# Loads of the up weights: from ScalarE's DMA queue to SyncE's

## The chip, the cores and the metric

The kernel runs on one core of a Trainium2 chip. The metric is the device time in microseconds (us) of one execution. Engines are named as in the profile: PE is TensorE, DVE is VectorE, ACT is ScalarE, POOL is GpSimd, SP is SyncE. SP does no arithmetic here; it issues DMA transfers. ACT computes and can issue DMA transfers as well. "SPq" and "ACTq" mark what an engine's sequencer does, such as issuing a transfer.

## What is computed

The reference has two parts: a causal linear attention with decay, and a two-layer network on its output.

```
# q, k, v: (4, 8, 768, 64) float32; lam: (8,)
for b in range(seq // 64):                      # blocks of 64 tokens
    intra = einsum('bhic,bhjc->bhij', qb, kb) * Dmask        # Dmask = lam ** (i - j), causal
    intra = einsum('bhij,bhjd->bhid', intra, vb)
    inter = einsum('bhid,bhde->bhie', qb * lam_pow, kv_state)
    out[:, :, block] = intra + inter
    kv_state = lam_block * kv_state + einsum('bhsd,bhse->bhde', kb * rev_pow, vb)
x = out.transpose(0, 2, 1, 3).reshape(3072, 512)
h = x @ w_in                                    # w_in: (512, 2048)
return maximum(0.01 * h, h) @ w_out             # w_out: (2048, 512)
```

w_in and w_out come in as 64-bit floats, everything else as 32-bit floats. "Up" is the product with w_in, "down" the product with w_out.

## The kernel before

**Attention.** Tokens are handled in 24 rounds of 128 (two blocks of the reference). A round loads k, q and v (`load_kq` L330, `load_v` L374), transposes k and q on PE (L391), copies the transposes out of PSUM on ACT (L402 for k, L403 for q), multiplies q and k by powers of lam (L411, L407), forms scores and the state update on PE (psc, by the helper at L312), masks the scores on DVE (L440), adds the state (L445, L447) and forms the output (po, again L312). The output is then split into three numbers, `xh`, `xl` and `xm` (L495 to L498), because the later products are made of three fast passes. k, q and v have two buffers each, so a load of round c + 2 waits for the PE work of round c. In the early rounds PE also makes filler transposes (`busy`, L265), a fixed number that the planner inserts.

**Weights.** The columns of w_in are taken in eight panels of 256. Each panel comes in two halves of 512 KB, so there are 16 loads; they go in turn into three staging buffers `raw`. Panels are taken in the order 1, 0, 2, 3, 7, 6, 5, 4, so loads 1 and 2 are panel 1, 3 and 4 panel 0, 5 and 6 panel 2. `to_float32` (L544) converts a half from 64 to 32 bits: its `get` issues the load, three ACTIVATEs (L566, L568, L570) read the staging buffer, and two DVE operations (L572, L573) put the words together in `w32`. `parts` (L575) then splits the panel into `wh`, `wl` and `wm` (L579 or L581, L584, L590). A staging buffer is free again when its three ACTIVATEs are done. The same function loads w_out later, from SP's queue.

**Up and down.** `up` (L616) multiplies a group of 512 tokens by a panel in three passes (L628), corrects and applies the leaky ReLU on ACT (L646, L649), and stores the result in device memory (L652, `g<-gs`). When all is done, `down` reads it back and makes the second product (L688).

**Order of the work.** The order on each engine isn't written by hand. `Plan` (L37) holds every operation with an estimated duration and its dependences, simulates the engines together with one resource "DMA", and emits the operations in order of their planned start. A load is planned on "DMA" by `move` (L278); which engine's queue issues it is settled only in the function that is then called. An engine works through its instructions in the emitted order. Transfers that SP issues go into SP's queue, those that ACT issues into ACT's queue.

Transfers take eight completion counters in turn, over both queues. A transfer waits on its issuing engine until the former transfer on its counter has landed; it also waits for the last reader of what it overwrites.

Of the kernel before, what the change touches and what calls it, by code (L numbers as in the profile page):

```python
# [36 lines left out]
class Plan:  # L37
# [23 lines left out]
    def add(self, eng, us, fn, reads=(), writes=(), rank=0.0):  # L61

        n, deps = len(self.ops), set()
        for k in reads:
            w, r = self.last.setdefault(k, [None, []])
            if w is not None:
                deps.add(w)
            r.append(n)
        for k in writes:
            w, r = self.last.setdefault(k, [None, []])  # L70
            if w is not None:
                deps.add(w)
            deps.update(r)
            self.last[k] = [n, []]
        deps.discard(n)
        ways = {eng: us} if isinstance(eng, str) else dict(zip(eng, us))
        if self.slack:
            self.more[n] = self.slack
        if self.chain is not None:
            self.chains[self.chain].append(n)  # L80
        self.ops.append((ways, fn, deps, (self.rank + rank, n), set(writes)))
# [81 lines left out]
def kernel(  # L163
# [10 lines left out]
    nc = tc.nc  # L174
# [103 lines left out]
    def move(us, fn, reads, writes, issue=0.5, rank=0.0, slack=SLACK):  # L278

        plan.slack = slack if steady else EARLY_SLACK  # L280
        if steady and not rank:
            rank = FIRST
        add("DMA", length(us, issue), fn, reads, writes, rank=rank)
        plan.slack = 0.0
# [259 lines left out]
    def to_float32(kind, p, h, dst, key, after=()):  # L544

        nonlocal n_raw
        j, n_raw = n_raw % (1 if kind == "wo" else len(raw)), n_raw + 1
        r, low, kl = raw[j], lows[n_raw % 2], f"low{n_raw % 2}"
        d = dst.bitcast(I32)

        def get():
            r64 = r.bitcast(I64)
            if kind == "wi":
                nc.scalar.dma_start(out=r64.rearrange("p (k f) -> p k f", k=2),
                                  in_=w_in_r[:, 2 * h:2 * h + 2, p * 2 * P:(p + 1) * 2 * P])
            else:
                nc.sync.dma_start(out=r64, in_=moe_w_out[(2 * p + h) * P:(2 * p + h + 1) * P, :])

        def words(i, dt):
            return r.bitcast(dt).rearrange("p (n two) -> p n two", two=2)[:, :, i]  # L560

        def addend(dt, i):
            return low.bitcast(dt).rearrange("p (n two) -> p n two", two=2)[:, :, i]

        move(1.6, get, after, [f"raw{j}"])
        add("ACT", 0.67, lambda: nc.scalar.activation(out=dst, in_=words(1, F32), func=AF.Abs, scale=2.0 ** -110),  # L566
            [f"raw{j}"], [key])
        add("ACT", 0.78, lambda: nc.scalar.activation(out=addend(U16, 0), in_=words(0, U32), func=AF.Copy, bias=0.0, scale=2.0 ** -29),  # L568
            [f"raw{j}"], [kl])
        add("ACT", 0.77, lambda: nc.scalar.activation(out=addend(F16, 1), in_=words(1, F32), func=AF.Copy, bias=0.0, scale=2.0 ** -100),  # L570
            [f"raw{j}"], [kl])
        add("DVE", 0.42, lambda: nc.vector.tensor_scalar(d, d, 3, None, op0=ALU.logical_shift_left), [], [key])  # L572
        add("DVE", 1.0, lambda: nc.vector.tensor_tensor(d, d, low, op=ALU.add), [kl], [key])  # L573
# [230 lines left out]
```

## Time and profile before

| what | value |
|---|---|
| median of 3 runs | 612.86 us (612.70 to 613.33) |
| the profiled execution's own time | 614.14 us |
| its span, first to last instruction | 612.3 us |
| PE busy | 600.5 us, 98% of the span |
| DVE, ACT, POOL busy | 312.2, 270.9, 83.0 us |
| moved by DMA | 104.66 MB, 171 GB/s on average |
| the 16 loads of w_in | issued from 7.0 to 79.0 us, 374 ns median to issue, 4.0 to 6.4 us to land |

A row of the profile names a group of instructions: line, engine, operation, output <- input, sizes and count. In the order of time a row begins with its start and duration in us; in brackets at its end stands how long the engine had been idle before and what ended that. Matmuls are pipelined and their ends are modelled. "Landing" is the end of a transfer, counted from the start of its issue. The chain that ended last is followed back from the last instruction, at each step to what released it. The names of tiles leave buffer numbers out: `raw` is any of the three staging buffers, and `att` is one large tile that holds nearly all of the attention's buffers.

### The profile page before, as it was taken

How to read it: one execution, taken by the hardware profiler on the slowest of the kernel's cores; microseconds unless marked ns; L12 is line 12 of the kernel's file. 1: busy time of each engine (PE TensorE's matmuls, PEld its weight loads, DVE VectorE, ACT ScalarE, POOL GpSimd, SP SyncE). 2: the span in 40 equal slices, each digit the busy share in tenths (PEclk: the TensorE clock that was granted, in tenths of full speed). 3: DMA queues.
4: the chain of work that ended last, by engine and by line, in shares of the span. 5: the costliest groups of instructions: out<-in, count | busy, mean ns of one | idle time of the engine just before them, and what ended most of it. 6: DMA issues, size and time to landing. Idle time of an engine off the chain costs nothing.

```text
span 612.3 us, 12915 instructions
## 1 busy us (share of the span) xinstructions
PE 600.5 (98%) x5402; PEld 498.1 (81%) x5402; DVE 312.2 (51%) x412; ACT 270.9 (44%) x434; POOL 83.0 (14%) x90
## 2 busy tenths in 40 slices
PE   8899999999999999999999999999999999999997
PEld 6677888888888888888788888888888888888886
DVE  3899981064353344326356845535454554635531
ACT  2778884444465655556577522221222313214111
POOL 1563410053233013103000000000000000000000
PEclk9999999999999999999999999999999999999999
DMA  9999876544889969876776842523433343433201
GB/s 205 219 248 255 237 205 169 152 123 131 192 207 253 234 192 244 219 237 172 287 263 223 286 161 88 187 70 126 149 101 122 120 135 106 138 103 121 86 1 69
DMA packets 141162, 104.66 MB, mean 171 GB/s; under 512 B 117040, under 2 KB 117808, under 8 KB 141104
## 3 DMA queue, kind: packets, MB, share of 16 engines
q1 hardware_dynamic: 136608, 95.44, 53.7%
q10 hardware_dynamic: 4496, 8.39, 4.5%
q8 instruction: 42, 0.69, 0.5%
q14 instruction: 16, 0.13, 0.1%
HBM read 68.16 MB, written 35.65 MB: 170 GB/s over the span
## 4 chain that ended last, share of the span: by engine, by line
PE 93%; DVE 4%; DMA 1%; POOL 1%; issue 0%; SPq 0%; ACT 0%; DVEq 0%; ACTq 0%; POOLq 0%
PE b L628 41%; PE b L688 18%; PE po L688 11%; PE psc L688 11%; PE po L312 4%; PE pt L688 4%; PE psc L312 3%; DVE w L572 1%; DVE w L573 1%; DMA att<-in_v_dram 1%; PE pt L391 1%; DVE wm L590 0%; DVE att L447 0%; DVE wl L584 0%; DVE wh L581 0%
## 5 line engine op out<-in xcount | busy, mean ns | idle before, releaser
L670 ACT ACTIVATE xh<-att 128x1024 fp32r<-128x1024 f32 x48 | 50.9, 1061 | 147.1 <-PE b L688 145.4
L671 DVE SCALAR_TENSOR_TENSOR xl<-att,xh 128x1024 fp32r<-128x1024 f32 x48 | 58.7, 1223 | 99.0 <-ACT xh L670 99.0
L628 PE MATMUL b<-xl,wl 128*128 128x512 f32 (+1 forms) x392 | 102.9, 386 | 0.6 <-DVE wl L584 0.6
L628 PE MATMUL b<-xh,wh 128*128 128x512 f32 (+1 forms) x392 | 102.7, 386 | 0.8 <-ACT xh L495 0.8
L628 PE MATMUL b<-xm,wm 128*128 128x512 f32 (+1 forms) x392 | 103.2, 391 | 0.0
L628 PEld LDWEIGHTS b<-xh,wh 128*128 128x128 f32 x392 | 72.7, 188 | 16.1 <-ACT xh L495 0.9
L628 PEld LDWEIGHTS b<-xl,wl 128*128 128x128 f32 x392 | 72.5, 188 | 15.7 <-DVE wl L584 1.0
L628 PEld LDWEIGHTS b<-xm,wm 128*128 128x128 f32 x392 | 71.3, 188 | 14.6
L649 ACT ACTIVATE gs<-b 128x512 f32<-128x512 f32 x96 | 57.2, 597 | 47.9 <-PE b L628 44.1
L646 ACT ACTIVATE b<-b 128x512 f32<-128x512 f32 x96 | 56.0, 585 | 50.4 <-PE b L628 50.3
L688 PE MATMUL b<-wl,xl 128*128 128x512 f32 x192 | 74.7, 389 | 0.0
L688 PE MATMUL b<-wh,xh 128*128 128x512 f32 x192 | 74.7, 389 | 0.0
L673 DVE SCALAR_TENSOR_TENSOR xm<-xl,xh 128x1024 fp32r<-128x1024 f32 x48 | 58.8, 1226 | 5.1 <-DVE xl L671 0.5
L440 DVE TENSOR_TENSOR att<-psc,att 128x512 f32<-128x512 f32 x24 | 16.5, 689 | 64.6 <-PE psc L312 64.5
L688 PEld LDWEIGHTS b<-wl,xl 128*128 128x128 f32 x192 | 36.1, 188 | 7.5
L688 PEld LDWEIGHTS b<-wh,xh 128*128 128x128 f32 x192 | 36.0, 188 | 7.5
L407 POOL TENSOR_TENSOR att<-att 128x512 f32<-128x512 f32 (+1 forms) x23 | 25.8, 1123 | 100.7 <-PE po L391 55.2
L450 POOL TENSOR_TENSOR att<-att 128x256 f32<-128x256 f32 x40 | 32.8, 820 | 45.7 <-DVE att L447 45.7
L572 DVE TENSOR_SCALAR w<-w 128x512 int32<-128x512 int32 x32 | 18.2, 569 | 39.5 <-ACT w L566 39.5
L688 PE MATMUL po<-wl,xl 128*128 128x512 f32 x96 | 37.4, 390 | 0.0
L688 PE MATMUL psc<-wh,xh 128*128 128x512 f32 x96 | 37.4, 389 | 0.0
L688 PE MATMUL psc<-wm,xm 128*128 128x512 f32 x96 | 37.4, 389 | 0.0
(73 smaller groups left out, 812.1 us busy)
## 6 DMA issues: line engine op xcount, KB each, us to landing
att<-g SPq DMA_DIRECT2D x48, 512.0 KB, 3.3
g<-gs SPq DMA_DIRECT2D x47, 512.0 KB, 3.9
raw<-in_moe_w_in_dram ACTq DMA_DIRECT2D x16, 512.0 KB, 4.9
raw<-in_moe_w_out_dram SPq DMA_DIRECT2D x16, 512.0 KB, 4.6
att<-in_k_dram SPq DMA_DIRECT2D x48, 128.0 KB, 4.6
att<-in_v_dram SPq DMA_DIRECT2D x24, 256.0 KB, 4.4
out_dram<-gs SPq DMA_DIRECT2D x23, 256.0 KB, 2.0
wo<-w SPq DMA_DIRECT2D x8, 512.0 KB, 5.7
```

The source lines that it names most:

```text
L312: nc.tensor.matmul(dst[HALF[cols]], lhsT=lhsT[HALF[rows]], rhs=rhs[HALF[rows]], start=start, stop=True, skip_group_check=True)
L407: lambda e="POOL": ENG[e].tensor_tensor(kr[nr], kr[nr], _bc(pow_k, 3, D)[nr], op=ALU.mult), ["fk"], [f"k{i}"])
L440: add("DVE", 0.69, lambda: nc.vector.tensor_tensor(sc, psc[:, :, lower, :], decay, op=ALU.mult), ["psc", "fk"], ["sc"])
L450: add("POOL", 0.7, lambda new=new, j=j: nc.gpsimd.tensor_tensor(state[(j + 1) % 4], new, _bc(lam_c, 2, D), op=ALU.mult), [f"st{j % 4}", "f ...
L572: add("DVE", 0.42, lambda: nc.vector.tensor_scalar(d, d, 3, None, op0=ALU.logical_shift_left), [], [key])
L628: nc.tensor.matmul(dst, lhsT=w[z][:, kk * 2 * P + f * P:kk * 2 * P + (f + 1) * P], rhs=x[z][:, kk, toks], start=start and kk == 0, stop=kk ...
L646: add("ACT", ns, lambda b=b: nc.scalar.activation(out=b, in_=b, func=AF.Copy, bias=0.0, scale=S + 1.0), [], [kb], rank=-1.5)
L649: add("ACT", ns, lambda b=b, r=r: nc.scalar.activation(out=r, in_=b, func=AF.Prelu, bias=0.0, scale=1.0 / WS, alpha=0.01), [kb], [f"gs{jg} ...
L670: add("ACT", 1.05, lambda: nc.scalar.activation(out=h, in_=graw[j], func=AF.Copy, bias=0.0, scale=NEAR), reads, wr("h"))
L671: add("DVE", 1.25, lambda: nc.vector.scalar_tensor_tensor(l, graw[j], 1.0, h.bitcast(F32), op0=ALU.mult, op1=ALU.subtract), reads + [f"rh{ ...
L673: add("DVE", 1.25, lambda: nc.vector.scalar_tensor_tensor(m, l.bitcast(F32), -S, h.bitcast(F32), op0=ALU.mult, op1=ALU.add), [f"rh{j}", f" ...
L688: nc.tensor.matmul(acc[tb][z // 2][:, cols], lhsT=ring[j][z][:, f * T + tb * P:f * T + (tb + 1) * P], rhs=W[pp][z][:, f * d_model:(f + 1) ...
```

## The change

The 16 loads of w_in are issued by SP (`nc.sync`) where ACT (`nc.scalar`) issued them. Source, destination, size, number of loads and their place in the plan stay as they are.

```diff
         def get():
             r64 = r.bitcast(I64)
             if kind == "wi":
-                nc.scalar.dma_start(out=r64.rearrange("p (k f) -> p k f", k=2),
+                nc.sync.dma_start(out=r64.rearrange("p (k f) -> p k f", k=2),
                                   in_=w_in_r[:, 2 * h:2 * h + 2, p * 2 * P:(p + 1) * 2 * P])
             else:
                 nc.sync.dma_start(out=r64, in_=moe_w_out[(2 * p + h) * P:(2 * p + h + 1) * P, :])
```

In the compiled program the instructions of PE, DVE and POOL keep their order. ACT's list loses the 16 issues and keeps its order otherwise; SP's list gains them. On SP they stand so: load 1 between v of round 1 and q of round 2; load 2 between k and v of round 2; load 3 between v of round 3 and k of round 4; load 4 between v of round 4 and k of round 5; loads 5, 6 and 7 in a row between q of round 7 and k of round 6; the others between later loads and stores of `g`.

## The prediction

> **What bounds the kernel now.** I read the page first, then the table by stage, then the chain that ended last over its first 60 us, and last the order of time around the first weight load. The page, engines and the load that moves:
>
> ```profile
> PE 600.5 (98%) x5402; PEld 498.1 (81%) x5402; DVE 312.2 (51%) x412; ACT 270.9 (44%) x434; POOL 83.0 (14%) x90
> ...
> raw<-in_moe_w_in_dram ACTq DMA_DIRECT2D x16, 512.0 KB, 4.9
> ```
>
> TensorE is busy 98% of 612.3 us. Only 11.8 us are idle; the time moves only if those do, or if the matmuls' own time does. Where they lie (us; busy time of PE, PEld, DVE, ACT, POOL with counts; clock, DMA share, GB/s):
>
> ```profile
> 0.00:10.00 10.00, 7.33 (x61) 5.72 (x61) 4.00 (x19) 2.46 (x3) 0.74 (x7) 1.00 0.88 176
> 10.00:20.00 10.00, 8.93 (x214) 7.38 (x213) 5.27 (x10) 4.87 (x11) 3.27 (x5) 1.00 0.89 219
> 20.00:30.00 10.00, 8.02 (x277) 6.52 (x276) 8.88 (x15) 7.24 (x13) 6.25 (x7) 1.00 1.04 238
> 30.00:40.00 10.00, 8.72 (x127) 6.78 (x119) 9.76 (x12) 6.77 (x13) 6.19 (x5) 1.00 1.02 250
> ...
> 60.00:70.00 10.00, 10.00 (x160) 8.86 (x159) 9.44 (x14) 8.56 (x16) 5.41 (x5) 1.00 0.89 257
> ```
>
> Of the idle time 7.6 us lie in the first 60 us (the six stages' busy times sum to 52.4), and none from 60 to 280; the rest is past the last of these loads. There VectorE rises to over 90% and, from 20 to 40 us, the DMA engines are full (1.04, 1.02). After 60 us TensorE doesn't wait. The 16 loads are issued between 7.0 and 79.0 us: those after 51 us can only matter if they come late enough to make TensorE wait again.
>
> The chain at its start (start us, us, what):
>
> ```profile
> 2.88 4.11 DMA att<-in_v_dram
> 7.44 0.59 ACT att L403
> 8.07 1.14 PE psc L312 x32
> 9.21 0.83 PE b L265 x3
> 10.04 1.06 PE psc L312 x32
> ...
> 49.54 1.15 DVE wl L584
> 50.73 3.02 PE b L628 x12
> ```
>
> The odd step is the second: L403 copies the transposed q of the first round out of PSUM and reads no v. The order of time shows why v is there:
>
> ```profile
> 5.55 1.06 PE L391 MATMUL pt<-att 128*128 128x128 f32 x4
> 6.41 0.85 PE L265 MATMUL b<-att 128*128 128x128 f32 x3
> 7.01 0.38 ACTq L554 DMA_DIRECT2D raw<-in_moe_w_in_dram  x1
> 7.44 0.59 ACT L403 COPY att<-pt 128x512 f32<-128x512 f32 x1 [1.48 <-DMA att<-in_v_dram]
> 8.07 1.14 PE L312 MATMUL psc<-att 64*64 64x64 f32 x32 [0.82 <-ACT att L403]
> ```
>
> Its input was ready at 6.61 (5.55+1.06). In front of it in ScalarE's order stands the first weight load. In the compiled program the loads take eight completion counters in turn, and this one takes the counter of the first v load, so it waits until that has landed (2.88+4.11 = 6.99), then issues for 0.38 us; the copy comes at 7.44 and TensorE idles 0.82 us. This is on the chain that ends last.
>
> **What the skill says.** "DMA: Bandwidth & Descriptors", section "Issuing engines are not separate DMA queues": DMAs issued by any engine run on the same 16 DMA engines, and issuing from several "will only save the time on the sequencer it takes to initiate the DMA". The trace agrees on the size (374 ns median on ScalarE) but shows more than that price: the wait before it. The same page, "Anatomy of one DMA", says that semaphore waits are made on the issuing sequencer before dispatch; the 7.01 row, 0.02 us after the v landing, agrees. Its "Queues, rings and completion order" gives SP and ACT one row each, served in turn by packet. The trace agrees: weight load 3, issued at 19.90 on ACT, lands at 24.6, beside q's first half issued at 18.70 on SP (24.5). "TensorE: Matmul & The Clock Gate", "What's actually happening", says that the clock doubles after a busy window of about 3.4 us, and that the windows run free. Here matmuls of L391 take 421 ns up to some 14 us and 272 ns after.
>
> **The change part by part.**
>
> *Taken from ScalarE: 16 issues x 0.374 = 6.0 us of its sequencer, and its waits.* Most is hidden. The load at 12.19 follows a copy that began at 12.18, and the next, L479, waits for TensorE until 13.89; at 19.90, 25.61, 31.73, 32.47 and 42.57 the issue lies under a running or waiting ACTIVATE. From 51 us on the cover is TensorE's unbroken work. Without it these issues would cost up to 0.4 us each. Only the first is uncovered: L403 can start at 6.61+0.04 (the usual gap: 14.85 to 14.89 in the next round) = 6.65 in place of 7.44, a gain of 0.79. Behind it TensorE has three filler transposes to 7.26, so scores start at about 7.28: again 0.79. VectorE's L411 (8.05, behind L403) moves with it. Keys and values of the round are in (6.99, 8.2); so the whole first chain moves.
>
> *Added to SP: 16 issues of 0.37 to 0.55 us, in order among q, k, v loads and g stores.* Load 1 comes after v of round 1 (6.18+0.55), delaying q of round 2 by some 0.5 us to about 12.5 to 13.1 at landing, against a first use at 17.77. Load 2 stands between k and v of round 2, and v waits for TensorE until 13.48. Later loads wait on SP until ScalarE has read their staging buffer. Behind load 10 (about 52.1) stands q, issued at 54.43; behind load 12 (60.7) q at 63.95; behind load 14 (71.6) a g store at 72.59. The next loads were waiting for TensorE or ScalarE anyway. So the block costs nothing; without that cover it would be up to 2 us on k, which lands only 0.4 to 0.9 us ahead of its transposes at 44.12, 53.59 and 63.10. There the weights now queue behind k instead of being served in turn with it, so k comes earlier.
>
> *Moved: the landings.* Bytes stay equal. Nine 128 KB pieces landed from 4.0 to 9.3 us: 0.59 us each. From 29.7 to 39.8 us ten such pieces (5.9) and about 2.3 weight loads landed: 1.8 us per weight load. On one queue loads 5 and 6 go behind q of round 7, which landed at 39.8 with both ahead of it. With their 3.6 us taken out q lands at 36.2, load 5 at 38.0 (before: 35.7), load 6 at 39.8 (38.9). Less the 0.8 that the chain has moved: 37.2 and 39.0. Their readers:
>
> ```profile
> 38.09 0.79 ACT L568 ACTIVATE low<-raw 128x512 uint16<-128x512 uint32 x1
> ...
> 41.88 1.22 ACT L566 ACTIVATE w<-raw 128x512 f32<-128x512 f32 x2
> ```
>
> Moved by 0.8, the readers need load 5 at 37.3 and load 6 at about 41.7: just enough, and ScalarE idles 0.95 us before L649 at 39.83, so another 0.9 us of lateness is covered. Load 4 by the same count comes at about 31.0, needed at 32.4-0.8 = 31.6. Loads 7 to 16 have 2 to 5 us, except the last (issued near 80.9 in place of 79.03; read at 86.4, landing near 84.5). In return q of round 4 and v of round 3 land 1 to 2 us sooner. Cost taken: 0; bounds: -0.3 (v no longer at 26.2, close to the 26.37 start of round 3) and +2.1 (second rival).
>
> *Clock.* If the clock doubles at the same moment, some 0.8 us of work now falls before it at half speed: about 0.1 to 0.2 lost.
>
> Sum: -0.79 +0 +0.15, about -0.65 to -0.8; I take -0.75. Against the profiled execution (614.14, span 612.3) 613.4 and span 611.55; its 1.28 above the median of the runs (612.86) is carried over, so 612.1.
>
> **Rivals.**
> 1. *The clock opens a window earlier.* The switch near 14.3 puts earlier window edges near 10.9 and 7.5. In 7.5 to 10.9 TensorE idled 0.57 us (7.5 to 8.07); with the move it idles none. If that window counts as busy, the forty matmuls at 12.29 take about 0.8 for 1.56 and the two sets of transposes 0.66 for 1.1 each: 1.2 to 1.6 more, so 610.8. Against it: free windows differ from run to run.
> 2. *Slower: weights late.* If the one queue loses as much as it gains by order, so that q of round 7 still lands at 39.8, load 5 lands at 41.6 and L568 is 3.5 late. After the 0.95 of cover and some 0.5 of spare on the accumulator banks, 2.1 reach VectorE's up-weight chain and the wait at 50.73. That gives 612.86+2.1-0.8 = 614.2, and more if k and q are late too. It decides from load 5 landing at about 39.5. For it: the DMA engines are full there, and SP's issues already stall (1 to 3 us per pair at 28.80 and 32.81). Against: less stands ahead of q.
> 3. *The gain is swallowed.* Filler, VectorE (9.76 of 10 busy from 30 us) or q of round 4 hold the chain at its old times: 612.8. For it: VectorE's work from 33 us has almost no gap. Against: its inputs come from the chain itself.
> That the load doesn't change queue is excluded: it is on SP in the compiled order.
>
> **Chances.** The forecast (0.7 to 0.8 carried) 0.38; clock 0.22; late weights 0.20; swallowed 0.20. The measurement can tell about 0.2%, 1.2 us: faster is below 611.6, slower above 614.1. The forecast is inside that; a tenth of it, with small gains elsewhere, falls below. The clock rival is nearly all faster; of late weights a little stays inside, and a little of the others is above. So faster 0.31, same 0.44, slower 0.25. The range takes in the clock case at its low end and late weights at 614.2 with a margin for more: 610.6 to 614.8; the likeliest case's own is 611.5 to 612.6.
>
> **What would show it.** L403 at about 6.65 without the v wait, L312 at about 7.28; the chain's first step no longer v. The twelve matmuls of L628 at about 49.95 in place of 50.73. Weight loads on SP, load 5 landing at 37 to 39. Matmuls at 272 ns from 11 us would show the clock rival; a new wait of TensorE or ScalarE for raw between 28 and 51 us the late weights. Wrong would make it above all a queue that moves less when it carries everything.

## The result and the profile after

The changed kernel takes 611.73 us (median of 8 runs, 610.70 to 612.44) against 613.21 us of the kernel before beside it (8 runs, 612.70 to 615.30). The ratio on record is 0.9968, with a 95% interval of 0.9954 to 0.9981: faster, by about 0.3%. Measured once more, beside the experiments, it was 612.08 us against 612.80, ratio 0.9986 (0.9975 to 0.9996). The medians lie 1.5 and 0.7 us apart, somewhat less than the ratios say (2.0 and 0.9 us). So the gain is real in both and lies near 0.2%, 1.2 us; its size is known to about half of itself. The profiled execution took 611.72 us with a span of 609.9, 2.4 us under the span before (612.3). The profiled execution before (614.14 us) was a long one, so differences of the two profiles are larger than those of the medians.

The page of the changed kernel, engines and the load that moved:

```profile
PE 598.7 (98%) x5402; PEld 496.0 (81%) x5402; DVE 312.6 (51%) x412; ACT 270.3 (44%) x434; POOL 83.2 (14%) x90
...
raw<-in_moe_w_in_dram SPq DMA_DIRECT2D x16, 512.0 KB, 5.7
```

TensorE's idle time is 11.2 us (609.9-598.7) where it was 11.8, but its busy time fell too, by 1.8 us, with the same 5402 matmuls. So part of the gain isn't a wait removed: the same matmuls ran in less time. The order of time from 5 to 9 us of the changed kernel:

```profile
5.50 1.06 PE L391 MATMUL pt<-att 128*128 128x128 f32 x4
...
6.35 0.85 PE L265 MATMUL b<-att 128*128 128x128 f32 x3
...
6.60 0.58 ACT L403 COPY att<-pt 128x512 f32<-128x512 f32 x1 [0.69 <-PE pt L391]
6.73 1.12 SPq L554 DMA_DIRECT2D raw<-in_moe_w_in_dram  x1
...
7.23 1.14 PE L312 MATMUL psc<-att 64*64 64x64 f32 x32
...
8.30 0.57 PE L265 MATMUL b<-att 128*128 128x128 f32 x3
```

L403 now waits for the transposes of q and for nothing else, and starts 0.84 us sooner. The scores follow at 7.23, and TensorE has no idle time ahead of them. The last row is new in kind: three filler transposes take 0.57 us, where the three at 6.35 take 0.85.

The same work a little later, first before, then after (order of time):

```profile
12.29 1.56 PE L312 MATMUL po<-att 64*64 64x64 f32 x40
...
13.78 1.07 PE L391 MATMUL pt<-att 128*128 128x128 f32 x4
...
16.68 1.16 PE L312 MATMUL psc<-att 64*64 64x64 f32 x64 [1.07 <-DVE att L447]
```

```profile
10.31 0.93 PE L312 MATMUL po<-att 64*64 64x64 f32 x40
11.17 0.65 PE L391 MATMUL pt<-att 128*128 128x128 f32 x4
...
13.65 1.16 PE L312 MATMUL psc<-att 64*64 64x64 f32 x64 [1.07 <-DVE att L447]
```

The lead grows from 0.84 us at the first scores to 3.03 at those of the next round, because the matmuls in between, output and transposes among them, run at the faster clock. The trace's record of the granted clock lists nothing for the slow start; it begins with the full clock, at 14.68 us before and at 8.40 us after. The durations of the rows agree.

The chain that ended last over its first 60 us, after:

```profile
0.74 3.26 DMA att<-in_k_dram
4.04 1.23 PE b L391 x4
5.28 0.43 PE b L265 x2
5.71 0.85 PE pt L391 x4
6.56 0.64 PE b L265 x3
7.23 1.14 PE psc L312 x32
```

v is no longer its first step: the chain begins with the first k and goes on with TensorE itself.

### The profile page after: what moved, and what is told of

It reads as the page before. It is cut to its first block, busy times and chain, and to the rows that moved or that the text cites. A ratio compares the mean times of both kernels' runs of the same rounds, so it can differ in the third digit from the quotient of the medians.

```text
span 609.9 us, 12921 instructions
## 1 busy us (share of the span) xinstructions
PE 598.7 (98%) x5402; PEld 496.0 (81%) x5402; DVE 312.6 (51%) x412; ACT 270.3 (44%) x434; POOL 83.2 (14%) x90
## 4 chain that ended last, share of the span: by engine, by line
PE 94%; DVE 3%; DMA 1%; ACT 1%; SPq 0%; issue 0%; DVEq 0%
PE b L628 42%; PE b L688 18%; PE po L688 11%; PE psc L688 11%; PE psc L312 4%; PE po L312 4%; PE pt L688 4%; PE pt L391 1%; PE po L391 1%; DMA att<-in_k_dram 1%; DMA raw<-in_k_dram 0%; DVE att L440 0%; DVE att L411 0%; DVE att L447 0%; DVE w L572 0%; DVE wm L590 0%
## 5 line engine op out<-in xcount | busy, mean ns | idle before, releaser
L572 DVE TENSOR_SCALAR w<-w 128x512 int32<-128x512 int32 x32 | 17.0, 530 | 40.8 <-ACT w L566 40.8
L688 PE MATMUL psc<-wl,xl 128*128 128x512 f32 x96 | 37.3, 389 | 0.0
```

What stands on the lines that cost most here:

```text
L688: nc.tensor.matmul(acc[tb][z // 2][:, cols], lhsT=ring[j][z][:, f * T + tb * P:f * T + (tb + 1) * P], rhs=W[pp][z][:, f * d_model:(f + 1) ...
```

## The experiments

Two moments serve as marks, since the order of VectorE's instructions is the same in all these kernels: the first L572 (19.69 us before) and the sixth L590, the last step of splitting a panel (77.14 before). "Clock" is where the trace's record of the full clock begins. "Fell" counts the executions whose mean granted clock is 0.997 or less; what that means is said under e7. Ratios are to the kernel before on the same chip, with 95% intervals. A mark is one execution, a ratio many. The experiments ask three questions in turn: whether it is load 1 in front of the first copy, whether it is the clock, and whether it is the landing of q, k and v.

| kernel | loads issued by ScalarE | L403 | clock | L572 | L590 | fell | ratio |
|---|---|---|---|---|---|---|---|
| before | all | 7.44 | 14.68 | 19.69 | 77.14 | 23 of 148 | |
| r_before | all | 7.40 | 11.80 | 18.41 | 76.06 |  | |
| after | none | 6.60 | 8.40 | 16.66 | 74.05 | 0 of 8 | 0.9968 (0.9954 to 0.9981) |
| r_after | none | 6.61 | 9.52 | 17.15 | 74.09 | 2 of 9 | 0.9986 (0.9975 to 0.9996) |
| e1_first_act | 1 | 7.41 | 12.73 | 18.80 | 75.59 | 1 of 14 | 0.9985 (0.9974 to 0.9996) |
| e2_first_sp | 2 to 16 | 6.46 | 8.04 | 16.46 | 75.35 | 9 of 13 | 0.9999 (0.9991 to 1.0007) |
| e5_after_copy | all, load 1 behind L403 | 6.43 | 4.96 | 16.02 | 74.87 | 6 of 13 | 0.9994 (0.9985 to 1.0003) |
| e3_fill | all | 7.38 | 10.05 | 17.82 | 75.42 | 4 of 21 | 0.9999 (0.9992 to 1.0005) |
| e6_one_three_sp | 2, 4 to 16 | 6.61 | 9.01 | 16.96 | 74.62 | 19 of 22 | 1.0007 (0.9997 to 1.0016) |
| e7_three_act | 3 | 6.58 | 8.44 | 16.67 | 76.19 | 5 of 13 | 0.9997 (0.9987 to 1.0006) |
| e8_order_on_act | all, 1 and 3 later | 6.48 | 7.68 | 16.31 | 75.33 | 8 of 13 | 1.0009 (1.0000 to 1.0018) |
| f1_four_sp | 5 to 16 | 6.21 | 5.06 | 15.80 | 73.53 | 8 of 22 | 0.9983 (0.9975 to 0.9991) |
| e4_gap | none | 6.64 | 12.76 | 18.39 | 75.85 | 0 of 22 | 0.9992 (0.9983 to 1.0000) |
| e9_warm | none | 6.32 | 5.44 | 15.91 | 73.71 | 3 of 14 | 0.9978 (0.9966 to 0.9990) |

**Is it load 1 in front of the copy?** Three kernels part the first load from the others. All compute the whole result.

e1_first_act and e2_first_sp (one line each):

```diff
-                nc.scalar.dma_start(out=r64.rearrange("p (k f) -> p k f", k=2),
+                (nc.scalar if (p, h) == (1, 0) else nc.sync).dma_start(out=r64.rearrange("p (k f) -> p k f", k=2),    # e1
+                (nc.scalar if (p, h) != (1, 0) else nc.sync).dma_start(out=r64.rearrange("p (k f) -> p k f", k=2),    # e2
```

> Load 1 is issued by ScalarE as before, loads 2 to 16 by SP as after. Theory W (the copy L403 waiting behind load 1 is the whole cause, with what follows from it): the time of the kernel before, ratio 0.999 to 1.001, L403 at about 7.4 us, TensorE idle about 0.8 us ahead of the first scores. Rival Q (one queue, and ScalarE freed of 15 issues, bring a good part): ratio 0.998 or lower although L403 starts at 7.4.

> Only load 1 is issued by SP, loads 2 to 16 by ScalarE as before. Theory W: the whole gain of the change, ratio 0.996 to 0.998, L403 at about 6.6 us. Rival Q: less than half of the gain, ratio 0.9985 or higher.

e5_after_copy keeps the queue and swaps two neighbours in ScalarE's order:

```diff
-                add("ACT", 0.6, lambda: nc.scalar.copy(qTs[i], pt), ["pt"], [f"qT{i}"])
+                add("ACT", 0.6, lambda: (nc.scalar.copy(qTs[i], pt), held and held.pop()()), ["pt"], [f"qT{i}"])
 ...   # left out: get() of load 1 puts its dma_start into held instead of issuing it
```

> All 16 loads stay on ScalarE; load 1 is issued one instruction later, behind the first copy L403. Theory W: what counts is that nothing stands ahead of L403, not the queue; ratio 0.996 to 0.998, L403 at about 6.6 us, load 1 issued at about 7.0 as before. Rival Q: ratio 0.9985 or higher.

Theory W, that the copy's wait is the whole cause, fails. With load 1 on SP alone, L403 starts at 6.46, as promised, and L572 comes 3.2 us sooner; yet the time doesn't move (0.9999). The swap on ScalarE gives the same picture (3.7 us sooner at L572, 0.9994). And with load 1 left in front of the copy, the other 15 loads on SP bring 0.9985. The lead is made early and lost later. Where, the order of time of e2_first_sp shows (the row of the kernel before at the same scores stands first):

```profile
26.37 0.92 PE L312 MATMUL psc<-att 64*64 64x64 f32 x47 [0.25 <-POOL att L407]
```

```profile
22.34 0.44 PE L391 MATMUL b<-att 128*128 128x128 f32 x2 [1.69 <-DMA att<-in_k_dram]
...
25.46 1.16 PE L312 MATMUL psc<-att 64*64 64x64 f32 x64 [0.51 <-DMA att<-in_v_dram]
```

TensorE waits 2.2 us for k and v of round 3; the kernel before shows no such wait in its first profile and 0.41 us for v in r_before. In e2 k's second half is issued on SP's queue at 16.7 and takes 5.6 us to land (22.3), while load 3, four times as large and issued on ScalarE's queue at 17.68, takes 4.0 (21.7): it overtakes k.

**Is it the clock?** e3_fill puts three more filler transposes of TensorE ahead of the first scores of the kernel before; e4_gap takes the three out that stand there in the changed kernel.

```diff
     def busy(n):
+        calls.append(n)
-        for _ in range(n):
+        for _ in range(n + 3 if len(calls) == 3 else n):     # e3, on the kernel before
+        for _ in range(0 if len(calls) == 3 else n):         # e4, on the changed kernel
```

> The kernel before with three more filler transposes of TensorE ahead of the first scores, which fill its idle 0.82 us while L403 still waits to about 7.4. Theory C (the larger half of the gain is TensorE's clock, which opens sooner once that idle stretch is gone): clock switch at 8 to 11 us in place of 14.7, ratio 0.997 to 0.998. Theory F (when the clock opens is chance, or the wait alone counts): ratio 0.999 to 1.001, no gain.

> The changed kernel without the three filler transposes ahead of the first scores, so that TensorE idles some 0.8 us there again although L403 comes at 6.6 us. Theory C (the idle stretch decides when the clock opens): switch at 10.6 to 15 us in place of 8.4 and 9.5; half or more of the gain goes, ratio 0.9985 to 1.000. Theory F (the moment is chance): switch anywhere from 4 to 15 us, ratio as with the change, 0.997 to 0.9985.

The moment of the clock does follow the idle stretch (theory C), in both directions. With L403 still at 7.38, e3 opens at 10.05; with L403 at 6.64 but TensorE idle again, e4 opens at 12.76. The order of time of e4_gap:

```profile
6.64 0.58 ACT L403 COPY att<-pt 128x512 f32<-128x512 f32 x1 [0.69 <-PE pt L391]
7.28 1.13 PE L312 MATMUL psc<-att 64*64 64x64 f32 x32 [0.68 <-ACT att L403]
...
11.49 1.48 PE L312 MATMUL po<-att 64*64 64x64 f32 x40
12.90 0.66 PE L391 MATMUL pt<-att 128*128 128x128 f32 x4
```

Over all profiles: the four with the idle stretch open at 11.80 to 14.68 us, the nine in which L403 comes early and TensorE idles there 0.35 us at most at 4.96 to 9.52, and e3 at 10.05. They don't overlap, so theory F, chance alone, falls; within each group the moment still varies by 3 to 5 us. But the earlier clock of e3 buys nothing: it has a lead at L572 (1.9 us, or 0.6 against r_before) and no gain in time (0.9999).

**Is it the landing of q, k and v?** e6, e7 and f1 choose which loads ScalarE issues, in the same line as e1: e6 `nc.sync if (p, h) in ((1, 0), (0, 0)) else nc.scalar`, e7 `nc.scalar if (p, h) == (0, 0) else nc.sync`, f1 `nc.sync if p < 2 else nc.scalar`. e8 keeps all on ScalarE and holds load 1 back behind L403 and load 3 behind the next L495, by the means of e5.

> The changed kernel once more, for its time on the same chip as the next three and for a second moment of the clock switch. Every theory: ratio 0.996 to 0.998. If the switch near 8.4 us in its first profile was brought by the change, it is again between 8 and 9 us; if the moment is chance, it lies anywhere from 4 to 15 us.

> Only loads 1 and 3 are issued by SP. Theory L (the early gain of the first chain is kept only if v of round 3 lands sooner, and what keeps it late is load 3, served in turn with q and v from its own queue): ratio 0.996 to 0.998, v of round 3 landing by about 24.4 us. Rival M (the many later loads matter): ratio 0.9985 or higher.

> All loads on SP except load 3, which ScalarE issues. Theory L: most of the gain goes, ratio 0.999 or higher, and TensorE waits for v of round 3, which lands at 25 us or later. Rival M: nearly all of the gain stays, ratio 0.996 to 0.9975.

> All 16 loads stay on ScalarE; load 1 is issued behind the first copy L403 and load 3 behind the next ACTIVATE of L495, about 1 us later than before and after v of round 3 has been issued. If order alone counts: ratio 0.996 to 0.998 as with the change. If a load on a queue of its own overtakes q and v even when it is issued after them: ratio 0.9985 or higher, v of round 3 landing at 25 us or later.

e7 is the plainest case. One load of sixteen goes back to ScalarE and the gain is gone (0.9997). TensorE, order of time of e7_three_act:

```profile
20.99 0.44 PE L391 MATMUL b<-att 128*128 128x128 f32 x2 [0.53 <-DMA att<-in_k_dram]
...
25.52 1.77 PE L312 MATMUL psc<-att 64*64 64x64 f32 x56 [1.91 <-DMA att<-in_v_dram]
```

v of round 3 was issued at 19.13 and landed 6.3 us later; load 3, issued at 17.70, landed in 4.2. In the changed kernel the same places read:

```profile
23.33 0.44 PE L391 MATMUL pt<-att 128*128 128x128 f32 x2 [0.45 <-DMA att<-in_q_dram]
...
24.49 1.16 PE L312 MATMUL psc<-att 64*64 64x64 f32 x64 [0.72 <-DVE xl L496]
```

There v takes 5.1 us from 19.25 and is in at about 24.4, when the copy L403 (24.39) and L496 (24.36) end as well: TensorE idles 0.72 us, but v isn't alone in holding it. In r_after v does hold it, for 0.43 us. The intervals of e7 and r_after overlap; it is the groups as a whole, below, that part.

e7's row at 25.52 shows a second loss: 56 matmuls take 1.77 us, where 64 take 1.16 after the change. The granted clock had gone back to half for 3.41 us (busy time of PE, PEld, DVE, ACT, POOL with counts; clock, DMA share, GB/s):

```profile
22.10:25.51 3.41, 1.50 (x35) 0.95 (x26) 2.32 (x4) 2.58 (x5) 3.35 (x4) 1.00 1.04 191
25.51:28.92 3.41, 3.40 (x77) 2.96 (x81) 1.35 (x3) 0.97 (x2) 0.34 (x2) 0.50 0.97 238
```

e5's profile has the same from 18.62 to 22.03, behind 3.41 us with TensorE busy for 1.87; no other profile has it before the last matmul. So a late load costs its wait and can cost a stretch at half clock on top. One such stretch takes 0.0028 off the mean granted clock of 612 us, which is on record for every execution but those of the kernel before in the first measurement: 0.996 and 0.997 in these two profiles, 0.999 or 1.000 in the others. That gives the column "fell". It is highest in e6, e2 and e8, where loads are late, and low in e1 and e4. The executions with a fall are about 1 us longer: medians of 613.34 against 612.43 us in e2, 613.27 against 612.43 in e7, 612.47 against 611.16 in f1. It isn't the whole loss: without them e7 is 0.3 us under the kernel before without them, and r_after 1.1 us. And f1 keeps its gain with 8 of 22.

e6 contradicts theory L as I had put it: load 3 on SP isn't enough (1.0007). Load 4, issued by ScalarE at 22.89, probably does to the next q what load 3 did to v. Order of time of e6_one_three_sp:

```profile
29.04 0.67 PE L391 MATMUL pt<-att 128*128 128x128 f32 x4 [1.51 <-DMA att<-in_q_dram]
```

Its profile was the fastest of its 22 runs and one of the three without a fall of the clock, so its L590 in the table flatters it. e8 didn't test what it was meant to: load 3 was to come behind v, but the faster chain moved ScalarE ahead as well, and it was issued at 17.79, before v at 19.25; TensorE waited 1.60 us for v (up to 25.24). So a load issued truly behind v on ScalarE's queue stays untried.

The theory was mended (L2) and tested with loads 1 to 4 on SP:

> Loads 1 to 4 are issued by SP, 5 to 16 by ScalarE as before. Theory L2 (what keeps the gain is that none of loads 1 to 4 is served in turn with the q, k and v of rounds 3 to 5; later loads are hidden either way): the gain of the whole change, ratio 0.997 to 0.9985, no wait of TensorE for k, q or v over 0.6 us between 15 and 30 us. Rival M (later loads matter, too): ratio 0.999 to 1.001.

It holds: 0.9983, with no wait of TensorE for a load between 15 and 30 us. Loads 5 to 16 can stay on ScalarE. v of round 3 lands at 23.5, just ahead of the scores:

```profile
23.64 1.16 PE L312 MATMUL psc<-att 64*64 64x64 f32 x64 [0.64 <-DVE w L573]
```

**A version that might beat both.** e9_warm is the changed kernel with two more fillers at the very start (`n + 2 if len(calls) == 1 else n`), and r_before a second profile of the kernel before.

> The changed kernel with two more filler transposes at the start, which close the idle 0.5 us ahead of the first transposes of k. Theory C: the switch comes at 4.8 to 8.2 us; ratio to the kernel before 0.996 to 0.9975, a little faster than the change. If landings of q and v already limit the chain: as with the change, 0.997 to 0.9985, with a wait of TensorE for a load between 20 and 28 us. Theory F: the moment does not follow, from 4 to 15 us.

> The kernel before, for a second moment of its clock switch. Theory C: 11.5 to 15 us, as in its first profile (14.7) and in the kernel with only load 1 on ScalarE (12.7). Theory F: anywhere from 4 to 15 us.

The clock opens at 5.44 us and at 11.80 us, both as theory C had it. e9's ratio, 0.9978, lies between the two of the changed kernel, so a further gain isn't shown. The order of time of e9_warm shows what may stop it:

```profile
23.83 1.16 PE L312 MATMUL psc<-att 64*64 64x64 f32 x64 [1.48 <-DMA att<-in_v_dram]
```

Even on one queue v of round 3 is now late, by 1.48 us: with the clock this early a landing limits the chain again.

**What the runs say together.** The five ratios with the early copy but with load 3 or 4 on ScalarE (e2, e5, e6, e7, e8), and e3's with them, average 1.0001, and each interval reaches 1. With loads 2 to 4 on SP and the late clock (e1, e4) they are 0.9985 and 0.9992; with loads 1 to 4 on SP and the early clock (after, r_after, f1, e9) 0.9968, 0.9986, 0.9983 and 0.9978. That the landing order is needed is shown: no kernel with load 3 or 4 on ScalarE has a gain clear of nothing, and f1 and e6, which differ in loads 2 and 4 alone, have intervals that don't meet. That the early start and clock add about another 0.1% on top is only suggested, since the intervals are that wide and e1 and r_after come out alike.

## Why the prediction was right, and where not

The time fell inside the range (610.6 to 614.8), 0.4 us below the 612.1 forecast. Against the kernel before the forecast was 0.75 us of gain; the two measurements give 2.0 (0.9968) and 0.9 (0.9986). Its own terms, -0.79 and +0.15, sum to 0.64 of gain, so 0.75 was a little more than they gave. That the time came so close is in part luck: the starting point of 612.86 us, from three runs, became 613.21 with eight, the lead was nearly four times as large as reckoned, and part of it was lost again.

*Taken from ScalarE, load 1.* Right as a mechanism: L403 at 6.60 (forecast 6.65), scores at 7.23 (7.28), v gone from the chain. Wrong as the account of the gain: "so the whole first chain moves" is true up to 20 us, but e2 and e5 do this step alone and gain 0.0001 and 0.0006, which isn't clear of nothing. The 0.79 us was counted as if nothing later stood in its way.

*Moved: the landings.* The sizes were right: load 4 was put at 31.0 and landed at 31.1, load 5 at 37.2 and landed at 37.4, load 6 at 39.0 and landed at 38.9. With a lead of 2.8 us and not 0.8 that was no longer soon enough for ScalarE. The order of time of the changed kernel at the readers of loads 4 and 5:

```profile
31.09 0.67 ACT L566 ACTIVATE w<-raw 128x512 f32<-128x512 f32 x1 [1.45 <-DMA raw<-in_moe_w_in_dram]
...
37.48 0.79 ACT L568 ACTIVATE low<-raw 128x512 uint16<-128x512 uint32 x1 [2.08 <-DVE att L440]
```

ScalarE idled 1.45 us for load 4; the idle 2.08 us ahead of 37.48 are put down to VectorE, but load 5 landed 0.1 us before, so they may be load 5's. TensorE, the bound, has no idle stretch over 0.05 us from 31.77 to 175 us: the cover that the step had named held.

What failed in this step is the other half: that q of round 4 and v of round 3 land sooner was seen, and put at 0, at best -0.3. It decides whether any of the lead is kept: with load 3 on ScalarE (e7) TensorE waits 2.4 us for k and v, and in that profile runs at half clock for 3.41 us after. The third rival, the gain swallowed by something that holds the chain at its old times, describes the outcome of e2, e5, e7 and e8, though there late k and v hold it. It doesn't describe the changed kernel, where the move of all loads to one queue also put v ahead of load 3.

*Clock.* "If the clock doubles at the same moment" was the wrong branch. The first rival came true in the profile, at 8.40 us. Its grounds were only half right. It put the switch before at 14.3 us and earlier edges at 10.9 and 7.5; from the recorded 14.68 they are at 11.27 and 7.86. Between these TensorE idled 0.21 us ahead of the first scores and not 0.57: most of its 0.82 us lay ahead of 7.86. Its size was 1.2 to 1.6 and measured 2.2 (lead of 0.84 at 7.23, 3.03 at the second scores). Its chance of 0.22 was too low: every kernel with the early copy and its fillers in place opened before 9.6 us. The lead is still 3.09 us at 166 us. About 0.5 of it goes at the second row below, long past the loads of w_in, and the span ends 2.4 us shorter.

```profile
174.55 0.77 DVE L371 STREAM_TRANSPOSE att<-raw 128x256 f32<-128x256 f32 x2 [5.26 <-DMA raw<-in_k_dram]
...
176.04 0.69 PE L312 MATMUL psc<-att 64*64 64x64 f32 x32 [0.48 <-DVE att L371]
```

VectorE's transpose of a later k waits for its load, and TensorE for it; in the first profile before, TensorE has no idle time there. So a landing took part of the lead again, one that the prediction hadn't looked at.

*Added to SP.* Right. Loads 10 and 12 were issued at 48.98 and 57.56, with the next q at 51.34 and 60.86: nothing behind them was seen to be held up. Issuing cost SP more than ScalarE (460 ns median, 1.92 us at most, against 374), hidden likewise.

*Late weights* (second rival) came in part, with the larger lead, but didn't reach TensorE: ScalarE idled 0.55 us for load 3 ahead of 25.89 and 1.45 for load 4, as above.

*What stays open.* How the gain splits between early start, clock and landings; and what exactly moves the clock. In each trace the changes of the granted clock lie whole multiples of 3.413 us apart (4, 1 and 172 of them in e5, 5, 1 and 171 in e7), and where these steps fall differs from one execution to the next; that alone can shift the opening by up to 3.4 us. How busy TensorE must be in a step isn't shown: f1 opened at 5.06 after one with 2.93 us busy, the changed kernel didn't at 4.99 after 2.90, and the kernel before didn't at 11.27 after 3.19. Nor is it shown for the fall, which came after 1.50 and 1.87 us (e7, e5), but not after 1.79 in e6.

## What to carry to other kernels

When a chain is made faster at its start, look up the landing times of what it uses next, in the profile, before the gain is booked: here nine leads of 2.5 to 3.9 us at 20 us (1.3 less against r_before) became 0.1% to 0.3%, or nothing. A transfer on a second queue doesn't wait its turn behind the first queue's transfers: in e2 load 3 was issued about 1 us after k's second half and landed 0.6 us ahead of it. Where those are more urgent, as here, putting all on one queue in the order of need can be worth more than the issue time it costs. When TensorE waits, look at the granted clock of the next microseconds too. And a single execution can't tell such kernels apart: the times of one kernel lay 2 to 4 us apart. A fall of the clock, about 1 us, is one cause; its first moment, 2.9 us apart in two profiles of the kernel before and 1.1 in two of the changed one, is probably another.

## What the hardware showed that was not expected

An idle stretch of 0.7 to 0.8 us of TensorE at 7 us put the full clock off by several microseconds (11.80 to 14.68 against 4.96 to 9.52 us); closing it with three useless transposes went with 10.05. The full clock can also be lost again within microseconds: in e7, after 3.41 us in which TensorE was busy for 1.50 and idled 1.91 at a stretch, it ran at half clock for 3.41 us. And issuing the same 512 KB load took 374 to 473 ns on ScalarE at every one of 16 places, but 367 to 1924 ns on SP; why is not shown.
